# Seven products for chunk 0 too, a fourth exponential buffer for the eighth pair, and a last store in halves

## The chip, the cores and the metric

The kernel runs on one core of a Trainium2 chip. The metric is the device time of one execution in microseconds (us). A core has five engines with a queue of instructions each: TensorE (PE; its weight loads are listed as PEld), VectorE (DVE), ScalarE (ACT), GpSimd (POOL) and SyncE (SP). SP, ACT and POOL also start transfers (DMAs). The time before is the median of five runs: 339.68 us (338.87 to 341.57).

## What is computed

Block-causal attention over 8 batches, 8 heads, 576 positions and 64 elements per head, followed by two large products with an activation between them:

```python
def _attn_ref(q, k, v):
    scores = (1.0 / np.sqrt(D)) * np.matmul(q, k.transpose(0, 1, 3, 2))
    mask = block_i >= block_j              # blocks of 64 positions
    scores = np.where(mask, scores, -1000000000.0)
    attn = np.exp(scores - np.max(scores, axis=-1, keepdims=True))
    attn = attn / (np.sum(attn, axis=-1, keepdims=True) + 1e-09)
    return np.matmul(attn, v)

x = attn_out.transpose(0, 2, 1, 3).reshape(4608, 512)
h = x @ w_in                               # 512 x 2048
g = h * (1.0 / (1.0 + np.exp(-beta * h)))
out = g @ w_out                            # 2048 x 512
```

## The kernel before

**Pairs.** The attention is done in 32 pairs of heads, four to a batch: pair u is batch u // 4. For each pair, Q and K are loaded, cast to bf16 and turned (batches 0 and 1 on TensorE, line 624, with a copy on DVE, line 632; later ones by a transposing DMA, line 660). Then come the scores on TensorE (line 692), the exponentials on ACT (lines 706 and 718) into a buffer of the class E, small memsets on DVE for the mask, the product with V on TensorE (line 744), the norm on DVE (lines 756 and 763), and a transpose into xT (batches 0 to 2 on TensorE, line 783, with copies on lines 791 and 793; later ones by DMA, line 770).

**Chunks.** The rest is done in nine chunks of 512 rows. Chunk r needs all pairs of the batches in which its rows lie: chunk 0 needs batch 0, chunk 1 batches 0 and 1, chunk 2 batches 1 and 2, and so on. Its hidden part has 16 groups of four products of 128x512 (line 955); after each group ACT takes the tanh (line 965) and DVE makes a slice of gT (line 969). The out part multiplies gT with w_out.

**Out part, plain.** Chunk 0 alone: four row blocks w, for each 16 products of 128x512 in one bank of PSUM (line 991), a copy by ACT (line 1006) and a store of 256 KB from the ACT queue (line 1012). Its products need w_out only as far as each has got.

**Out part, Strassen.** The chunks listed in FAST (line 378), 1 to 8, cut gT and w_out into quarters and take seven products of quarters instead of eight. Each of the seven is two halves of eight products of 128x256 (line 885). They need sums and differences of gT's quarters (line 852, eight instructions on DVE for a chunk, some in place, some in the tensor OV) and of w_out's (function weights, line 832, eight instructions, once; one quarter of w_out is changed in place, after all plain products). OV shares its memory with a buffer for V of batch 1, so these also wait for that buffer's casts. The results are gathered in three accumulators, Z, W and Y, one bank of PSUM each: ACT copies out of Z (line 900) and DVE adds to the copy from W or Y (line 903). Four blocks are stored per chunk, 256 KB each, from the ACT queue (line 910).

**Buffers.** There are three E buffers (NE = 3). A fourth, of the class EX, lies in the memory of gT[1], the gT buffer of chunk 1; only pair 3 uses it (line 665). So the slices of chunk 1's gT wait for the users of that tile, which is remembered as `spare` (lines 733 and 971). PSUM has eight banks: scores take pairs of banks from (0, 2), the V product a pair from the list `pv.at` (line 736), and single tiles (P1) banks 4 to 7 while pairs are still to be placed, all eight afterwards.

**Order.** All work is entered as operations with dependences, buffers, an estimated duration and a priority. A planner (class Plan) plays them through in its own estimated time and fixes the order in each engine's queue: at each step the ready operation with the lowest priority number goes first. The number is 1000 + 100 r + j for hidden group j of chunk r; for Strassen halves 16 + 0.1 k above the chunk's base for the first two, and above 103 for the others, so that these lie among the next chunk's hidden groups; 10 u for pairs 4 to 7; and 994 + 100 (b - 1.5) + 4.9 c for pair c of a later batch b. `after` and `rest` of a store hold it back behind another operation or for a time. In the last chunk (`fin`) all halves follow at once.

Of the kernel before, what the change touches and what calls it, by code (L numbers as in the profile page):

```python
# [4 lines left out]
ACT = mybir.ActivationFunctionType  # L5
ALU = mybir.AluOpType
# [11 lines left out]
NRC = NROWS // RC  # L18
# [337 lines left out]
def bass_blockwise_causal_attn__then__act_swish_beta_kernel(  # L356
# [10 lines left out]
    with es:  # L367
# [7 lines left out]
        GROUPS = [((0,), (1,), (2,), (3,))] + [((0, 1), (2, 3))] * 7  # L375
        NS = 6
        NO = 4
        FAST = range(1, NRC)
        RX = 5 * RC
        OV = sb("OV", [128, 5120], f32)  # L380
        ST = [sb(f"ST{i}", [128, 36, 64], f32) for i in range(2)]
# [5 lines left out]
        TW = {k: OVh[:, k - 2] for k in (2, 3, 4)}  # L387
# [20 lines left out]
        ost = [sb(f"ost{i}", [128, DM], f32) for i in range(NO)]  # L408
        warm = sb("warm", [128, 2], f32)
        PS = es.enter_context(nc.psum_tensor("PS", [128, 8, 512], f32))  # L410
# [4 lines left out]
        P = Plan()  # L415
# [11 lines left out]
        def dve_t(n):  # L427
            return (n + 125) / 0.96
# [16 lines left out]
        def mk(fn):  # L445
# [4 lines left out]
            out=identF[:], in_=identF[:], compare_op=ALU.not_equal, fill=1.0, base=0,  # L450
# [3 lines left out]
            out=identB[:], in_=identB[:], compare_op=ALU.not_equal, fill=1.0, base=0,  # L454
# [5 lines left out]
        for i in range(NQ):  # L460
# [5 lines left out]
            o = P.op("POOL", 200, mk(lambda g, i=i: g.memset(Vn[i][:, 4, :, 64:66], 0.0)), prio=-5)  # L466
# [6 lines left out]
        for i in range(NQ, NE + 1):  # L473
# [4 lines left out]
                  xfer=100, dma=("d_beta", 1), prio=0.1)  # L478
# [28 lines left out]
        for i in range(NFILL):  # L507
# [10 lines left out]
            n = 215 if i < 12 else 110  # L518
            o = P.op("PE", n, ff, deps=[c2, c4], tiles=[tf], lat=n, mode="full", prio=1e6 + i)
# [6 lines left out]
        for b in range(B):  # L526
# [4 lines left out]
            for h0, h1, e, tt in PARTS[b]:  # L531

                vs = []
                for i in tt:
# [9 lines left out]
                    n = (h1 - h0) / 8 * (1 if i < 4 else 0.25)  # L544
# [46 lines left out]
        for u in range(NU):  # L591
            b, c = divmod(u, NPAIR)
# [69 lines left out]

                turned = [P.op("SP", 3250, ft, deps=casts, tiles=[tt_, tn], xfer=3200, prio=-1, dma=["d_T", 0, 1])]
            tqk, cps = tt_, turned
            te = P.tile("EX" if u == 3 else "E")
            ex = []
            zs = []
            qk = {}
# [61 lines left out]
                    a = 1024 * g0 + 512 * h + off + 128 * i - 128 * t  # L730
                return Ef[es_(te)][:, a:a + 128]

            if u == 3:
                spare = te
            pv = P.tile("PP")
            pv.at = (4, 6, 0, 2) if u == 3 else (4, 6) if b < 1 else (0, 2)
            ti, tx = P.tile("inv"), P.tile("xq")

            def fav(g, e, te=te, pv=pv, Tv=Tv, c=c):
# [98 lines left out]
        def fast(r, row, tg, gs):  # L838
            if not tw:
                weights()  # L840
            fin = r == NRC - 1
            old = [o for t in early for o in t.users] if r == FAST[0] else []
            t2, t3 = P.tile("S2"), P.tile("S3")
            NP = 2
            SZ = HJ // NP

            def G(a, b, i=None):
                x = gT[tg.slot][:, HJ * b:HJ * b + HJ, HC * a:HC * a + HC]
                return x if i is None else x[:, SZ * i:SZ * i + SZ]
# [13 lines left out]
            for i in range(NP):  # L863
                o = comb(lambda i=i: G(1, 0, i), lambda i=i: G(1, 0, i), lambda i=i: G(1, 1, i), ALU.add, i,
                         gs[SZ * i:SZ * i + SZ] + gs[HJ + SZ * i:HJ + SZ * i + SZ] + [SS[3][i]], [tg])
                o.same = gs[SZ * i:SZ * i + SZ] + gs[HJ + SZ * i:HJ + SZ * i + SZ]
                SS[3][i].same = gs[SZ * i:SZ * i + SZ]
                SS[1].append(o)
            for i in range(NP):
                o = comb(lambda i=i: piece(SW[2], i), lambda i=i: G(1, 0, i), lambda i=i: G(0, 0, i), ALU.subtract, i,  # L870
                         [SS[1][i]] + old, [tg, t2])
                o.same = [SS[1][i]]
                SS[2].append(o)

            def out_rows(a, b):
                return out[row + HC * a:row + HC * a + HC, HM * b:HM * b + HM].rearrange("(w p) n -> p w n", p=128)

            step = [0]

            def prod(ps, fa, fb, deps, tiles, first, last):  # L880
                z = []
                for w in range(2):
                    def fp(g, e, w=w):
                        for j in range(HJ):
                            x = g.matmul(PS[:, ps.slot, HM * w:HM * w + HM], fa()[:, j, 128 * w:128 * w + 128],  # L885
                                         fb()[:, j, :], start=first and w == 0 and j == 0, stop=last and w == 1 and j == HJ - 1,
                                         skip_group_check=True)
                        return x

                    k = step[0]  # L890
                    step[0] += 1
                    n = HJ * mm(HM)
                    z.append(P.op("PE", n, fp, deps=deps, tiles=[ps, tg, *tiles], lat=n + 170, mode="full",
                                  prio=1000 + 100 * r + (16 + 0.1 * k if fin or k < 2 else 103 + 16 / 12 * (k - 2))))
                z[1].after = z[0]
                return z

            def evac(ps, to, deps, add=None, same=()):
                if add is None:
                    return P.op("ACT", act_t(DM) + 80, lambda g, e: g.activation(  # L900
                        ost[to.slot][:], PS[:, ps.slot, :], ACT.Copy, scale=0.5),
                        deps=deps, tiles=[ps, to], lat=act_t(DM) + 160, prio=0)
                o = P.op("DVE", dve_t(DM), lambda g, e: g.scalar_tensor_tensor(  # L903
                    out=ost[to.slot][:], in0=PS[:, ps.slot, :], scalar=0.5, in1=ost[add.slot][:],
                    op0=ALU.mult, op1=ALU.add), deps=deps, tiles=[ps, to] + ([add] if add is not to else []), prio=0)
                o.same = list(same)
                return o

            def store(to, a, b, x, after=None, rest=0.0):
                o = P.op("ACT", 500, lambda g, e: [g.dma_start(  # L910
                    out_rows(a, b), ost[to.slot][:].rearrange("p (w n) -> p w n", w=2))],
                    deps=[x], tiles=[to], xfer=900, dma=["d_ost", to], prio=-1)
                o.after, o.rest = after, rest
                return o

            Z, W, Y = P.tile("P1"), P.tile("P1"), P.tile("P1")
            oz, ou, ot, oc = (P.tile("ost") for _ in range(4))
            wl, wh = wout[0:2], wout[2:4]
            lo, hi = gs[0:HJ], gs[HJ:NJ]
            p1 = prod(Z, lambda: G(0, 0), lambda: quad(w_out, 0, 0), lo + wl, [], True, False)  # L920
            z1 = evac(Z, oz, p1)
            p2 = prod(W, lambda: G(0, 1), lambda: quad(w_out, 1, 0), hi + wh, [], True, True)
            c11 = evac(W, oz, p2 + [z1], add=oz)
            for i in range(NP):
                o = comb(lambda i=i: G(0, 1, i), lambda i=i: G(0, 1, i), lambda i=i: piece(SW[2], i), ALU.subtract, i,
                         [SS[2][i]] + p2 + hi, [tg, t2])
                o.same = [SS[2][i]] + hi
                SS[4].append(o)
            p6 = prod(Z, lambda: SW[2], lambda: TW[2], SS[2] + tw[2] + [z1], [t2], False, False)
            u2 = evac(Z, ou, p6)  # L930
            store(oz, 0, 0, c11, after=u2)
            p7 = prod(Y, lambda: SW[3], lambda: TW[3], SS[3] + tw[3], [t3], True, False)
            p5 = prod(Z, lambda: G(1, 0), lambda: quad(w_out, 0, 1), SS[1] + tw[1] + [u2], [], False, False)
            tt = evac(Z, ot, p5)
            c22 = evac(Y, ot, p7 + [tt], add=ot)
            p3 = prod(Z, lambda: G(0, 1), lambda: quad(w_out, 1, 1), SS[4] + [tt] + wh, [], False, True)
            c12 = evac(Z, oc, p3)
            store(oc, 0, 1, c12)
            store(ot, 1, 1, c22, after=c12)
            p4 = prod(Y, lambda: G(1, 1), lambda: TW[4], hi + tw[4] + [c22], [], False, True)  # L940
            c21 = evac(Y, ou, p4 + [u2], add=ou)
            store(ou, 1, 0, c21, rest=0.0 if fin else 1500.0)

        for r in range(NRC):
            row = RC * r
# [139 lines left out]
```

## Time and profile before

| | |
|---|---|
| median of five runs | 339.68 us |
| profiled execution | 339.68 us, of which the span of instructions 337.9 |
| granted TensorE clock | 1.00 |
| hidden products, 128x512 (L955) | 576 |
| chunk 0's out products, 128x512 (L991) | 64 |
| Strassen products, 128x256 (L885) | 896 |
| ACT tanh, 128x512 (L965) | 144 of 697 ns |
| ACT exponential, 128x1024 (L706) | 96 of about 1.03 us |
| stores (ACT queue) | 36 of 256 KB |

An instruction is named by engine, line and the tiles that it writes and reads. A matmul's listed duration runs from its start to its modelled end, so that neighbours overlap; the rate of a stream is read from the chain of waits or from start to start. The chain of waits is followed back from the last instruction to what released each step. In the list of stretches each engine's busy time stands with the number of its instructions.

### The profile page before, as it was taken

How to read it: one execution, taken by the hardware profiler on the slowest of the kernel's cores; microseconds unless marked ns; L12 is line 12 of the kernel's file. 1: busy time of each engine (PE TensorE's matmuls, PEld its weight loads, DVE VectorE, ACT ScalarE, POOL GpSimd, SP SyncE). 2: the span in 40 equal slices, each digit the busy share in tenths (PEclk: the TensorE clock that was granted, in tenths of full speed). 3: DMA queues.
4: the chain of work that ended last, by engine and by line, in shares of the span. 5: the costliest groups of instructions: out<-in, count | busy, mean ns of one | idle time of the engine just before them, and what ended most of it. 6: DMA issues, size and time to landing. Idle time of an engine off the chain costs nothing.

```text
span 337.9 us, 7534 instructions
## 1 busy us (share of the span) xinstructions
PE 328.3 (97%) x3162; PEld 206.5 (61%) x3106; DVE 222.6 (66%) x447; ACT 211.5 (63%) x314; POOL 86.1 (25%) x127
## 2 busy tenths in 40 slices
PE   7998999999999999999999999999999999999995
PEld 5575446535567556865566666567556766666684
DVE  3737867487864679737957695768376866666742
ACT  1762994189467788559777659775777545544511
POOL 7646181084083007301530352051000000000000
PEclk9999999999999999999999999999999999999999
DMA  8999999999999799999899999997021200110023
GB/s 196 223 238 228 191 223 199 191 267 214 188 247 203 163 206 207 180 187 224 165 162 229 251 199 222 195 145 159 33 53 39 83 31 33 50 45 31 23 73 126
DMA packets 154978, 53.43 MB, mean 158 GB/s; under 512 B 139056, under 2 KB 154432, under 8 KB 154944
## 3 DMA queue, kind: packets, MB, share of 16 engines
q1 hardware_dynamic: 140096, 39.14, 61.1%
q10 hardware_dynamic: 9280, 9.44, 8.8%
q0 software_dynamic: 5568, 4.36, 8.2%
q8 instruction: 25, 0.41, 0.5%
q14 instruction: 9, 0.07, 0.1%
HBM read 36.71 MB, written 9.44 MB: 137 GB/s over the span
## 4 chain that ended last, share of the span: by engine, by line
PE 91%; ACT 4%; DVE 3%; issue 1%; POOL 0%; POOLq 0%; ACTq 0%
PE PS L955 35%; PE PS L885 29%; PE PS L744 8%; PE PS L692 8%; PE PS L991 4%; PE PS L513 2%; ACT E L706 2%; DVE gT L969 2%; PE PS L515 2%; PE PS L783 1%; ACT th L965 1%; PE PS L624 1%; DVE xq L763 1%; DVE gT L852 1%; ACT xT L791 0%
## 5 line engine op out<-in xcount | busy, mean ns | idle before, releaser
L955 PE MATMUL PS<-xT,w_in 128*128 128x512 bf16 x576 | 137.5, 380 | 0.6 <-ACT xT L791 0.2
L965 ACT ACTIVATE th<-PS,beta 128x512 f32<-128x512 f32 x144 | 96.7, 697 | 59.9 <-PE PS L955 59.1
L969 DVE SCALAR_TENSOR_TENSOR gT<-th,PS 128x512 f16<-128x512 f32 x144 | 95.6, 682 | 36.9 <-ACT th L965 36.6
L706 ACT ACTIVATE E<-PS 128x1024 bf16<-128x1024 f32 x93 | 92.3, 1029 | 28.0 <-PE PS L692 26.9
L955 PEld LDWEIGHTS PS<-xT,w_in 128*128 128x128 bf16 x576 | 52.7, 98 | 56.7 <-issue 3.4
L885 PE MATMUL PS<-w_out,gT 128*128 128x256 f16 x512 | 63.2, 273 | 0.0
L885 PEld LDWEIGHTS PS<-w_out,gT 128*128 128x128 f16 x512 | 48.9, 98 | 11.4 <-issue 0.2
L564 POOL CAST Vn<-Vs 128x640 bf16<-128x640 f32 (+1 forms) x28 | 21.0, 749 | 100.9 <-DMA Vs<-in_v_dram 99.6
L653 POOL CAST QKn<-ST 128x640 bf16<-128x640 f32 x48 | 38.8, 808 | 28.0 <-DMA ST<-in_k_dram 14.0
L692 PE MATMUL PS<-QKT 64*128 64x192 bf16 (+4 forms) x328 | 37.1, 297 | 0.7 <-DVE xq L763 0.6
L744 PEld LDWEIGHTS PS<-Vn,E 128*128 128x128 bf16 x930 | 31.7, 97 | 3.8 <-DVE xq L763 0.4
L900 ACT ACTIVATE ost<-PS 128x512 f32<-128x512 f32 x32 | 19.2, 599 | 23.5 <-PE PS L885 23.4
L744 PE MATMUL PS<-Vn,E 128*128 128x65 bf16 x930 | 32.8, 193 | 0.3 <-DVE xq L763 0.3
L885 PE MATMUL PS<-OV 128*128 128x256 f16 x256 | 32.0, 273 | 0.0
L692 PEld LDWEIGHTS PS<-QKT 64*128 64x128 bf16 (+1 forms) x328 | 13.4, 95 | 27.4 <-issue 15.4
L885 PEld LDWEIGHTS PS<-OV 128*128 128x128 f16 x256 | 24.3, 98 | 6.1 <-issue 0.4
L763 DVE TENSOR_TENSOR xq<-PS,inv 128x640 bf16<-128x640 f32 x32 | 26.3, 821 | 0.8
L903 DVE SCALAR_TENSOR_TENSOR ost<-PS,ost 128x512 f32<-128x512 f32 x24 | 16.3, 681 | 14.0 <-PE PS L885 8.4
L852 DVE TENSOR_TENSOR OV<-gT 128x1024 f16<-128x1024 f16 x32 | 23.3, 738 | 0.5
L712 DVE MEMSET E<- 64x64 uint32 x62 | 6.9, 112 | 23.9 <-ACT E L706 22.1
L885 PE MATMUL PS<-OV,gT 128*128 128x256 f16 x128 | 16.0, 273 | 0.0
L991 PE MATMUL PS<-w_out,gT 128*128 128x512 f16 x64 | 15.3, 380 | 0.0
(60 smaller groups left out, 178.7 us busy)
## 6 DMA issues: line engine op xcount, KB each, us to landing
out_dram<-ost ACTq DMA_DIRECT2D x36, 256.0 KB, 3.2
ST<-in_q_dram SPq DMA_DIRECT2D x12, 576.0 KB, 6.0
ST<-in_k_dram SPq DMA_DIRECT2D x12, 576.0 KB, 8.0
Vs<-in_v_dram SPq DMA_DIRECT2D x24, 256.0 KB, 4.3
ST<-in_q_dram SPq DMA_DIRECT2D x8, 288.0 KB, 7.3
ST<-in_k_dram SPq DMA_DIRECT2D x8, 288.0 KB, 7.7
w_in<-in_moe_w_in_dram POOLq DMA_DIRECT2D x4, 512.0 KB, 10.2
w_out<-in_moe_w_out_dram POOLq DMA_DIRECT2D x4, 512.0 KB, 9.9
```

Source lines behind the costliest of these rows:

```text
L564: return g.tensor_copy(Vn[t.slot][:, 0:n, g0:g1, 0:64], Vs[ts.slot][:, 0:n, g0:g1, :])
L653: return g.tensor_copy(QKn[tn.slot][:].rearrange("p a w n -> p (a w n)")[:, 640 * (2 * a + w):][:, 0:640] .rearrange("p (t h d) -> p t h d ...
L692: z = g.matmul(o, QKT[tqk.slot][r, p, 1, 128 * t + y:128 * t + m + y], x)
L706: return g.activation(E3[es_(te)][:, g0, :, :], PS[:, ps.slot:ps.slot + 2, :], ACT.Exp, scale=0.125)
L744: z = g.matmul(o, eblk(te, t, i, h), Vn[Tv.slot][:, t, 2 * c + h, 0:65], start=(t == 0), stop=(t == i))
L763: return g.tensor_tensor(xq[tx.slot][:].rearrange("p i (h d) -> p h i d", h=2), both(pv, 0, 64), x, ALU.mult)
L852: return P.op("DVE", dve_t(SZ * HC / 2), mk(lambda g: g.tensor_tensor(fo(), fx(), fy(), op)), deps=deps, tiles=tiles, prio=prio)
L885: x = g.matmul(PS[:, ps.slot, HM * w:HM * w + HM], fa()[:, j, 128 * w:128 * w + 128], fb()[:, j, :], start=first and w == 0 and j == 0, st ...
L955: z = g.matmul(PS[:, ph.slot, :], w_in[:, c, 128 * j:128 * j + 128], xT[:, c, row % RX:row % RX + RC], start=(c == 0), stop=(c == 3))
L965: return g.activation(th[tt.slot][:], PS[:, ph.slot, :], ACT.Tanh, scale=beta[:, j:j + 1])
L969: return g.scalar_tensor_tensor(out=gT[tg.slot][:, j, :], in0=th[tt.slot][:], scalar=1.0, in1=PS[:, ph.slot, :], op0=ALU.add, op1=ALU.mult)
L991: z = g.matmul(PS[:, po.slot, 0:d1 - d0], gT[tg.slot][:, j, 128 * w:128 * w + 128], w_out[:, j, d0:d1], start=(j == 0), stop=(j == NJ - 1))
```

## The change

The diff has three parts. FAST now begins with chunk 0, so all nine chunks use Strassen's seven products, and the combined weights are made before chunk 0's. Pair 7 too uses the class EX, `spare` becomes pair 7's tile, and pair 7's V product may take any of the four pairs of banks. In the last chunk Y is two tiles, one for each half of 256 columns: the sums out of it are done by halves (new function half), the last block is stored in two DMAs, and SP issues all its stores, without the order by `after`. The pause `rest` before the last store of chunk 7 goes to zero.

```diff
-        FAST = range(1, NRC)
+        FAST = range(0, NRC)
...
-            te = P.tile("EX" if u == 3 else "E")
+            te = P.tile("EX" if u in (3, 7) else "E")
...
-            if u == 3:
+            if u == 7:
                 spare = te
             pv = P.tile("PP")
-            pv.at = (4, 6, 0, 2) if u == 3 else (4, 6) if b < 1 else (0, 2)
+            pv.at = (4, 6, 0, 2) if u == 3 else (4, 6) if b < 1 else (0, 2, 4, 6) if u == 7 else (0, 2)
...
             def prod(ps, fa, fb, deps, tiles, first, last):
                 z = []
+                pair = isinstance(ps, list)
                 for w in range(2):
-                    def fp(g, e, w=w):
+                    pw = ps[w] if pair else ps
+
+                    def fp(g, e, w=w, pw=pw):
                         for j in range(HJ):
-                            x = g.matmul(PS[:, ps.slot, HM * w:HM * w + HM], fa()[:, j, 128 * w:128 * w + 128],
-                                         fb()[:, j, :], start=first and w == 0 and j == 0, stop=last and w == 1 and j == HJ - 1,
-                                         skip_group_check=True)
+                            x = g.matmul(PS[:, pw.slot, HM * w:HM * w + HM], fa()[:, j, 128 * w:128 * w + 128],
+                                         fb()[:, j, :], start=first and (pair or w == 0) and j == 0,
+                                         stop=last and (pair or w == 1) and j == HJ - 1, skip_group_check=True)
...
+            def half(ps, to, deps, add, w):
+                n = slice(HM * w, HM * w + HM)
+                return P.op("DVE", dve_t(HM), lambda g, e: g.scalar_tensor_tensor(
+                    out=ost[to.slot][:, n], in0=PS[:, ps.slot, n], scalar=0.5, in1=ost[add.slot][:, n],
+                    op0=ALU.mult, op1=ALU.add), deps=deps, tiles=[ps, to] + ([add] if add is not to else []), prio=0)
...
-            def store(to, a, b, x, after=None, rest=0.0):
-                o = P.op("ACT", 500, lambda g, e: [g.dma_start(
-                    out_rows(a, b), ost[to.slot][:].rearrange("p (w n) -> p w n", w=2))],
-                    deps=[x], tiles=[to], xfer=900, dma=["d_ost", to], prio=-1)
-                o.after, o.rest = after, rest
+            def store(to, a, b, x, after=None, rest=0.0, w=slice(0, 2)):
+                o = P.op("SP" if fin else "ACT", 500, lambda g, e: [g.dma_start(
+                    out_rows(a, b)[:, w], ost[to.slot][:].rearrange("p (w n) -> p w n", w=2)[:, w])],
+                    deps=[x], tiles=[to], xfer=450 * (w.stop - w.start), dma=["d_ost", to], prio=-1)
+                o.after, o.rest = None if fin else after, rest
...
-            Z, W, Y = P.tile("P1"), P.tile("P1"), P.tile("P1")
+            Z, W, Y = P.tile("P1"), P.tile("P1"), [P.tile("P1"), P.tile("P1")] if fin else P.tile("P1")
...
-            c22 = evac(Y, ot, p7 + [tt], add=ot)
+            c22 = [half(Y[w], ot, p7 + [tt], ot, w) for w in range(2)] if fin else [evac(Y, ot, p7 + [tt], add=ot)]
...
-            p4 = prod(Y, lambda: G(1, 1), lambda: TW[4], hi + tw[4] + [c22], [], False, True)
-            c21 = evac(Y, ou, p4 + [u2], add=ou)
-            store(ou, 1, 0, c21, rest=0.0 if fin else 1500.0)
+            p4 = prod(Y, lambda: G(1, 1), lambda: TW[4], hi + tw[4] + c22, [], False, True)
+            if fin:
+                for w in range(2):
+                    store(ou, 1, 0, half(Y[w], ou, [p4[w], u2], ou, w), w=slice(w, w + 1))
+            else:
+                store(ou, 1, 0, evac(Y, ou, p4 + [u2], add=ou), rest=1500.0 if r < NRC - 2 else 0.0)
```

More of the change, by code (lines that the diff above doesn't have):

```diff
@@ L892, in prod @@
                     n = HJ * mm(HM)
-                    z.append(P.op("PE", n, fp, deps=deps, tiles=[ps, tg, *tiles], lat=n + 170, mode="full",
+                    z.append(P.op("PE", n, fp, deps=deps, tiles=[pw, tg, *tiles], lat=n + 170, mode="full",
                                   prio=1000 + 100 * r + (16 + 0.1 * k if fin or k < 2 else 103 + 16 / 12 * (k - 2))))
@@ L938, in fast @@
             store(oc, 0, 1, c12)
-            store(ot, 1, 1, c22, after=c12)
-            p4 = prod(Y, lambda: G(1, 1), lambda: TW[4], hi + tw[4] + [c22], [], False, True)
-            c21 = evac(Y, ou, p4 + [u2], add=ou)
-            store(ou, 1, 0, c21, rest=0.0 if fin else 1500.0)
+            store(ot, 1, 1, c22[-1], after=c12)
+            p4 = prod(Y, lambda: G(1, 1), lambda: TW[4], hi + tw[4] + c22, [], False, True)
[4 more added lines that the diff above has]
+                store(ou, 1, 0, evac(Y, ou, p4 + [u2], add=ou), rest=1500.0 if r < NRC - 2 else 0.0)
         for r in range(NRC):
```

## The prediction

> **What bounds the kernel now.** I read the page's shares and slices first, then the chain of waits, then busy time by stretch, then the order of the instructions in two places: around pair 7, and at the end.
>
> ```profile
> span 337.9 us, 7534 instructions
> PE 328.3 (97%) x3162; PEld 206.5 (61%) x3106; DVE 222.6 (66%) x447; ACT 211.5 (63%) x314; POOL 86.1 (25%) x127
> ...
> DMA  8999999999999799999899999997021200110023
> ...
> PE 91%; ACT 4%; DVE 3%; issue 1%; POOL 0%; POOLq 0%; ACTq 0%
> ```
>
> TensorE carries 91% of the chain that ended last. The DMA slices are full up to about 230 us and then nearly empty: the attention inputs arrive at the pace of the transfers, chunks of the second part (hidden and out products) fill TensorE between the pairs, and what is left runs after them.
>
> ```profile
> 55.16 0.38 PE PS L692 x6
> 55.56 1.02 ACT E L706
> ...
> 57.72 2.70 PE PS L991 x12
> 60.42 0.90 PE PS L744 x30
> ...
> 68.69 2.59 PE PS L955 x12
> ...
> 320.33 13.99 PE PS L885 x128
> ```
>
> These are pieces of the chain: start, length, what. They give the rates of a full stream: 12 hidden products of 128x512 in 2.59 us, 216 ns each; 128 Strassen products of 128x256 in 13.99 us, 109.3 ns each. Around 55.56 the chain leaves TensorE for pair 7's exponential.
>
> ```profile
> 40.59 0.76 DVE L632 COPY QKT<-PS 128x576 bf16<-128x576 bf16 x1
> ...
> 50.56 1.97 PE L744 MATMUL PS<-Vn,E 128*128 128x65 bf16 x60
> ...
> 54.96 0.56 PE L692 MATMUL PS<-QKT 64*128 64x320 bf16 x6
> ...
> 60.25 1.07 PE L744 MATMUL PS<-Vn,E 128*128 128x65 bf16 x30
> ...
> 65.07 1.03 PE L955 MATMUL PS<-xT,w_in 128*128 128x512 bf16 x4
> ```
>
> Pair 7's turned Q and K lie ready at 41.35 (the last of the 16 copies of L632), but its scores start at 54.96: all three E buffers were held until pairs 4 and 5 had been multiplied with V (50.56 to 52.5). So its V product comes at 60.25 and chunk 1's hidden products start at 65.07. Until then TensorE lives on chunk 0's plain out products: 32 of 64 (4, 12, 8 and 8 in the timeline) lie before 65.07, 6.9 us.
>
> ```profile
> 40.00:50.00 10.00, 9.87 (x57) 4.13 (x52) 6.71 (x16) 9.50 (x16) 6.52 (x9) 1.00 1.13 213
> 50.00:57.00 7.00, 6.74 (x122) 4.59 (x120) 6.31 (x15) 3.10 (x5) 2.17 (x3) 1.00 1.23 205
> 57.00:65.00 8.00, 8.00 (x73) 4.19 (x69) 3.35 (x10) 1.94 (x2) 0.00 (x0) 1.00 1.25 196
> 65.00:80.00 15.00, 14.88 (x105) 6.70 (x101) 10.81 (x20) 11.21 (x18) 8.39 (x10) 1.00 1.07 245
> 80.00:95.00 15.00, 15.00 (x126) 8.10 (x121) 11.82 (x26) 10.34 (x15) 2.86 (x3) 1.00 1.10 197
> 95.00:110.00 15.00, 14.35 (x176) 10.88 (x171) 7.92 (x21) 9.14 (x15) 8.89 (x12) 1.00 1.10 219
> ```
>
> Busy us in each stretch (PE, PEld, DVE, ACT, POOL; clock, DMA share, GB/s): TensorE is full; ACT is nearly full only from 40 to 50, DVE has least room from 50 to 57 and from 65 to 95.
>
> **What the Trainium skill says.** TensorE: Matmul & The Clock Gate, "Back-to-back issue gap", gives N/2.4 + 2.5 ns for a warm array: 215.8 ns for 512 columns and 109.2 for 256. The trace agrees (216 and 109.3). DMA: Bandwidth & Descriptors, "Anatomy of one DMA — SWDGE (gpsimd) path", fits about 2.0 us of fixed cost to a DMA of the GpSimd path, most of it the receipt of the write, so halving a store can't halve its landing; this trace's late stores land in 2.2 to 2.6 us, of which my packet sum below leaves about 1.5 fixed. PSUM — Partial Sum Buffer, "PSUM bank collisions raise a hardware error", demands that a reader takes another bank than the matmul writes: that is why halves of the last sum need two banks. No run here shows a collision.
>
> **The change, part by part.**
>
> Chunk 0's products. Removed: 64 of 128x512, 64 x 216 = 13.8 us. Added: 7 x 16 = 112 of 128x256, 112 x 109.3 = 12.2 us. TensorE gains 1.6 us. DVE gains 8 combinations of 0.69 us (L852's median), 5.5 us, and 3 sums of 0.69 (L903), 2.1 us; ACT keeps 4 copies (0.60 each). Stores stay four of 256 KB. The eight weight combinations (L832, about 6 us) are only moved from in and behind chunk 0 to ahead of its later products: they need all of w_out, whose last quarter lands at 48.50 + 13.7 = 62.2. DVE from 50 to 110 holds about 40 us of work by the rows above; with 7.6 more it is at about 80%. Between 120 and 140, where Strassen chunks already run, it holds 16.1 of 20 us and TensorE is full there, so I price the load at nothing. What hides the wait for the combined weights is chunk 1's hidden work, 64 x 216 = 13.8 us of it; without that cover it costs what the slower rival below says.
>
> Pair 7's fourth buffer. Its scores can follow pair 6's, whose exponentials end at 47.47, instead of waiting for 52. Its three wide exponentials and the short one (3 x 1.02 + 0.22 = 3.3 us) then fall where ACT is busy 9.5 of 10 us (40 to 50), and push chunk 0's last five tanh back by as much, to about 56; ACT is nearly idle from 52 to 66, so it catches up. The V product follows pair 6's at about 54, its norm, transposes and copies take what they take now (60.25 to 63.96, 3.7 us), so xT is complete at about 58 and hidden chunk 1 starts some 7 us earlier. That stands in for the plain products as filler. TensorE's sum from 50 to 65 closes: four V products (3.6), transposes (1.6), four or five late hidden groups of chunk 0 (4), pair 7's scores gone, products 1 of Strassen (1.8, its two quarters of w_out landed at 52.1 and 55.4), and four or more hidden groups of chunk 1 (3.5 and more). The chain's step at 55.56 (1.0 us) goes; bounds: 1.0 gained, to 1.0 lost when the displaced tanh or DVE's longer queue leave gaps between 47 and 60. I take 0.2 gained. The wait that chunk 1's gT has on the alias of gT[1] moves from pair 3 to pair 7; chunk 1 needs pair 7's xT anyway, so it adds nothing.
>
> The end. Today:
>
> ```profile
> 333.72 1.73 ACTq L910 DMA_DIRECT2D out_dram<-ost x2
> 333.81 0.49 PE L885 MATMUL PS<-OV,gT 128*128 128x256 f16 x3
> ...
> 334.34 0.69 DVE L903 SCALAR_TENSOR_TENSOR ost<-PS,ost 128x512 f32<-128x512 f32 x1 [2.45 <-PE PS L885]
> ```
>
> Product 4 ends at 334.30, the sum takes 0.69, the store is issued at about 335.06, the span ends at 337.9. Split, the first half's sum and store run beside the second half's eight products (0.87 us). A 256-wide sum has no row; 512 takes 0.68 to 0.69 and 640 (L763) 0.82, a slope of about 1.1 ns per element, so about 0.40: 0.29 gained. A store's half is 128 packets of 1 KB; the page's q10 gives 8.8% x 16 x 337.9 / 9280 = 51 ns per packet, over 16 engines 0.41 us for 128: 0.41 gained. Bounds: nothing, if the landing is all fixed cost, to 0.7. SP takes over all four blocks' stores of the last chunk, five DMAs; its queue has nothing left but the wait for the stores (71.4 us of it in the list of waits), and each issue takes about 0.4, so the one for the first half (about 333.9) is out before the last (about 334.8). The other sum now takes two halves, about 0.1 longer, beside product 3. Total for the end: 0.7.
>
> The pause of 1.5 us before chunk 7's last store falls away: it moves one issue, worth nothing either way.
>
> Sum: 339.68 (the profiled execution: span 337.9 and 1.8 around it) - 1.6 - 0.2 - 0.7 = 337.2. The profiled execution is also the median of the five.
>
> **Rivals.** "Cannot be told from no change" is within 0.5%, 338.0 to 341.4.
>
> A, the attention sets the pace. Hidden chunk 2 starts at 109.28, when batch 2's last xT copy is done, and by then, counted in the timeline, 160 of the 176 out products of chunks 0 and 1 are through: 16, or 1.75 us, are in hand. Taking 1.6 us of work away leaves 0.15. If the pairs come no earlier and the remaining products wait for sums, TensorE idles instead, and only the end's 0.7 is won: 339.0. For it: full DMA slices. Against: 24 products in hand at chunk 3's start (145.4), 80 at chunk 4's, so only two places are tight, and pairs move up when TensorE is freer.
>
> B, slower. Pair 7 does not come forward (its scores are placed behind the V products because PSUM pairs, not E, hold it), and hidden chunk 1 still starts at 65. Until then only products 1 are free of combined weights; 6.9 us of filler are replaced by 1.75, 5.2 lost against 2.3 won: 342.6. It decides once chunk 1 starts later than about 61. Against: both score banks are free at 47.5, and its V product may use two more bank pairs.
>
> C, the front gains more: the gaps before 110 (0.65 us in the last row, some of the waits on ACT near 73) close as well; 335.5.
>
> **Numbers.** Forecast 0.64, A 0.15, B 0.13, C 0.08. The forecast's own range, with the end from 0 to 0.7 or a little more and the front 1.0 either way, is 335.8 to 338.9. The range 335.4 to 339.6 takes C and A in and leaves B and edges out. Faster by over 0.5%: four fifths of the forecast and C, 0.60; within: the rest of the forecast and A, 0.27; slower 0.13.
>
> **What would show it.** In the changed profile: L885 x1008 and no L991; pair 7's scores before 50; the first hidden product of chunk 1 near 58; no gap of TensorE over half a us between 55 and 75, and at 105 to 110; last matmul 1.6 to 2 us earlier; from it to the end about 2.9 instead of 3.6. I am wrong if hidden chunk 1 starts after 61, or if TensorE idles before chunk 2.

## The result

| | before | after |
|---|---|---|
| median of the compared runs | 339.6 us (337.4 to 343.1) | 340.43 us (338.47 to 342.86) |
| ratio, with 95% interval | | 1.0025 [1.0008, 1.0041] |
| profiled execution | 339.68 us, span 337.9 | 338.79 us, span 337.0 |

No gain. The time lies above the range (335.4 to 339.6), on the side that 0.27 was given to: within half a per cent. A second measurement of the same kernel, further down, gave 0.9992 [0.9966, 1.0018]. In every kernel some executions have a mean granted clock of 0.995 or less, instead of 0.998 or more, and mostly take 1 to 2 us longer; at full clock alone the second measurement is 339.45 us against 338.67, a ratio of 1.0023, close to the 1.0025 of the first.

So the changed kernel is not faster, and is probably about a quarter of a per cent slower.

The profiled execution is quicker than the median of its kernel by 1.6 us. It is one draw: chunk 0's hidden part begins at 31.0 us in it and at 31.9 in the profile of before, and in the profiles of all kernels below this start lies anywhere between about 30 and 32.5. So the profile tells where the time lies, and the medians how much it is.

The page of the changed kernel, the totals and the first line of its chain of waits:

```profile
span 337.0 us, 7638 instructions
PE 327.8 (97%) x3210; PEld 210.5 (62%) x3154; DVE 229.1 (68%) x460; ACT 211.8 (63%) x314; POOL 86.1 (26%) x127
...
PE 86%; DVE 7%; ACT 5%; issue 1%; POOL 0%; POOLq 0%
```

DVE's part of the chain rose from 3 to 7%, TensorE's fell from 91 to 86. DVE's busy time rose by 6.5 us only, 2% of the span. Where it rose is the point. Busy us by stretch in the changed kernel (PE, PEld, DVE, ACT, POOL; clock, DMA share, GB/s):

```profile
57.00:65.00 8.00, 7.78 (x51) 4.38 (x51) 7.55 (x18) 3.73 (x6) 0.00 (x0) 1.00 1.16 214
65.00:80.00 15.00, 14.45 (x134) 8.96 (x128) 14.33 (x24) 10.30 (x15) 9.95 (x11) 1.00 1.09 214
80.00:95.00 15.00, 14.24 (x138) 9.45 (x134) 10.55 (x22) 8.54 (x15) 1.90 (x3) 1.00 1.19 223
95.00:110.00 15.00, 14.84 (x205) 11.44 (x198) 8.84 (x23) 7.93 (x12) 8.28 (x11) 1.00 1.10 223
```

From 65 to 80 DVE is busy for 14.33 of 15 us, 96% (10.81 before), from 57 to 65 for 7.55 of 8 (3.35 before). TensorE, almost full there before (14.88 of 15), has holes. The timeline of the changed kernel shows two of them (start, length, engine, what; in brackets the idle time before and what ended it):

```profile
74.34 1.05 PE L888 MATMUL PS<-OV 128*128 128x256 f16 x8 [0.44 <-DVE OV L832]
...
77.05 2.23 POOL L653 CAST QKn<-ST 128x640 bf16<-128x640 f32 x2 [0.62 <-DMA ST<-in_q_dram]
77.49 1.20 DVE L832 TENSOR_TENSOR OV<-w_out,OV 128x1024 f16<-128x1024 f16 x1
77.60 1.07 PE L744 MATMUL PS<-Vn,E 128*128 128x65 bf16 x30
...
78.90 0.91 DVE L832 TENSOR_TENSOR OV<-w_out,OV 128x1024 f16<-128x1024 f16 x1
...
80.03 0.22 DVE L756 RECIPROCAL inv<-PS 128x10 f32<-128x10 f32 x1
80.28 0.82 DVE L763 TENSOR_TENSOR xq<-PS,inv 128x640 bf16<-128x640 f32 x1
...
81.75 0.53 PE L783 MATMUL PS<-identB,xq 128*128 128x128 bf16 x5 [0.76 <-DVE gT L981]
```

At 74.34 a product of chunk 0 waits for its combined weights. The second hole takes one step more to read. Pair 8's V product ends near 78.6. Its norm, which needs a fifth of a microsecond for the reciprocal, starts at 80.03, because two weight combinations (77.49 and 78.90) and two small memsets are ahead of it in DVE's queue. TensorE's queue has the transpose of that norm next and stands until 81.75. The wait ended with a slice of gT (L981, 81.02 to 81.70), which comes right behind the norm in DVE's queue: both are late by the two combinations ahead of them. In the kernel before, the V product of the same pair came at the same time, its norm followed at once, and the transpose had no wait:

```profile
77.49 1.07 PE L744 MATMUL PS<-Vn,E 128*128 128x65 bf16 x30
...
78.62 0.22 DVE L756 RECIPROCAL inv<-PS 128x10 f32<-128x10 f32 x1
...
80.25 0.52 PE L783 MATMUL PS<-identB,xq 128*128 128x128 bf16 x5
```

To compare kernels I added up all such holes of TensorE: each matmul counts with its own rate, the rest is wait, and matmul records missing from a trace are allowed for. These sums are estimates; the differences between kernels say more than the levels.

| TensorE waits, us | before | after | after, again |
|---|---|---|---|
| 40 to 57 | 1.3 | 1.9 | 2.5 |
| 57 to 95 | 1.8 | 3.9 | 4.5 |
| 95 to 110 | 1.8 | 1.3 | 1.3 |
| 40 to 110, sum | 4.9 | 7.1 | 8.3 |
| 110 to 270, sum | 7.2 | 7.3 | 7.2 |

TensorE's own work after 30 us fell from 284.2 to 282.0 us. The 1.6 us from chunk 0's products are in that. Between 40 and 110 the waits grew by 2.2 us, by 3.4 in the second profile, and take it back. Of this growth 0.6 and 1.2 us lie ahead of 57, where transposes of the last pairs wait for norms, and 2.1 and 2.7 between 57 and 95. From chunk 0's first hidden group to chunk 8's it is 266.6 us before, 267.4 and 268.4 after.

The end, in the timeline of the changed kernel:

```profile
332.35 1.91 PE L888 MATMUL PS<-OV,gT 128*128 128x256 f16 x16
...
333.42 0.42 DVE L903 SCALAR_TENSOR_TENSOR ost<-PS,ost 128x256 f32<-128x256 f32 x1 [1.51 <-PE PS L888]
334.29 0.42 DVE L903 SCALAR_TENSOR_TENSOR ost<-PS,ost 128x256 f32<-128x256 f32 x1 [0.45 <-PE PS L888]
```

The last product ends at 334.26 and the span 2.74 us later; before it was 334.30 and 3.6. So in these two executions the whole 0.9 us lies behind the last product, and nothing ahead of it, in spite of the earlier start.

### The profile page after: what moved, and what is told of

It is laid out like the page before. It is cut to its first block, busy times and chain, and to the rows that moved or that the text cites. A ratio compares the mean times of both kernels' runs of the same rounds, so it can differ in the third digit from the quotient of the medians.

```text
span 337.0 us, 7638 instructions
## 1 busy us (share of the span) xinstructions
PE 327.8 (97%) x3210; PEld 210.5 (62%) x3154; DVE 229.1 (68%) x460; ACT 211.8 (63%) x314; POOL 86.1 (26%) x127
## 4 chain that ended last, share of the span: by engine, by line
PE 86%; DVE 7%; ACT 5%; issue 1%; POOL 0%; POOLq 0%
PE PS L967 34%; PE PS L888 31%; PE PS L692 8%; PE PS L744 7%; PE PS L513 2%; ACT th L977 2%; ACT E L706 2%; DVE gT L981 2%; PE PS L515 1%; PE PS L783 1%; DVE xq L763 1%; DVE OV L832 1%; DVE OV L852 1%; DVE QKT L632 1%; PE PS L624 1%
## 5 line engine op out<-in xcount | busy, mean ns | idle before, releaser
L981 DVE SCALAR_TENSOR_TENSOR gT<-th,PS 128x512 f16<-128x512 f32 x144 | 96.2, 682 | 37.6 <-ACT th L977 36.6
L706 ACT ACTIVATE E<-PS 128x1024 bf16<-128x1024 f32 x90 | 89.1, 1027 | 25.1 <-PE PS L692 23.7
L888 PE MATMUL PS<-w_out,gT 128*128 128x256 f16 x576 | 71.4, 273 | 0.1
L888 PEld LDWEIGHTS PS<-w_out,gT 128*128 128x128 f16 x576 | 54.8, 98 | 13.8 <-issue 1.1
L909 ACT ACTIVATE ost<-PS 128x512 f32<-128x512 f32 x36 | 21.6, 601 | 33.7 <-PE PS L888 33.7
L888 PE MATMUL PS<-OV 128*128 128x256 f16 x288 | 36.5, 273 | 0.4 <-DVE OV L832 0.4
L744 PEld LDWEIGHTS PS<-Vn,E 128*128 128x128 bf16 x900 | 30.1, 97 | 4.3 <-ACT E L706 0.8
L888 PEld LDWEIGHTS PS<-OV 128*128 128x128 f16 x288 | 27.1, 98 | 8.0 <-issue 1.1
L852 DVE TENSOR_TENSOR OV<-gT 128x1024 f16<-128x1024 f16 x36 | 25.5, 719 | 1.7 <-PE PS L888 1.2
L888 PE MATMUL PS<-OV,gT 128*128 128x256 f16 x144 | 18.0, 273 | 0.0
L888 PEld LDWEIGHTS PS<-OV,gT 128*128 128x128 f16 x144 | 13.9, 98 | 2.5 <-issue 0.2
```

The lines of the kernel that those rows point to most:

```text
L706: return g.activation(E3[es_(te)][:, g0, :, :], PS[:, ps.slot:ps.slot + 2, :], ACT.Exp, scale=0.125)
L744: z = g.matmul(o, eblk(te, t, i, h), Vn[Tv.slot][:, t, 2 * c + h, 0:65], start=(t == 0), stop=(t == i))
L888: x = g.matmul(PS[:, pw.slot, HM * w:HM * w + HM], fa()[:, j, 128 * w:128 * w + 128], fb()[:, j, :], start=first and (pair or w == 0) and ...
L981: return g.scalar_tensor_tensor(out=gT[tg.slot][:, j, :], in0=th[tt.slot][:], scalar=1.0, in1=PS[:, ph.slot, :], op0=ALU.add, op1=ALU.mult)
```

## The experiments

Six theories, by the letters that the expectations use. **W**: DVE, loaded with sums and weight combinations ahead of chunk 0's products, makes TensorE wait, and that eats the saving. **P**: the attention sets the pace, so work taken from TensorE comes back as idle time wherever the pairs arrive (rival A). **X**: pair 7's early exponentials cost more than they bring. **T**: the stores by SP or the end in halves cost. **O**: any change of operations makes the planner write other queues, and each order has its own waits. **S**: one kind of such waits, norms torn apart: the planner leaves 70 ns between reciprocal and multiply, and a long DVE instruction gets in. Every set has its own runs of the kernel before (medians 339.12, 339.6 and 339.46 us).

### One part at a time

Strassen for chunk 0 alone, no fourth buffer for pair 7, end as before:

```diff
-        FAST = range(1, NRC)
+        FAST = range(0, NRC)
```

> Chunk 0 with seven products alone; pair 7 in an E buffer and the end as before. Theory W (the sums on DVE ahead of chunk 0's products make TensorE wait between 57 and 95 and eat the 1.6 us saved): ratio 0.999 to 1.005, waits of TensorE between 57 and 110 at least 1.5 us longer than before. Rival P (the attention sets the pace, the saving is lost at the starts of chunks 2 and 3 or later): 0.998 to 1.001, TensorE idle in front of the first hidden group of chunk 2 or 3. As predicted blind for this part: 0.995.

345.47 us, ratio 1.0187 [1.0156, 1.0219], slower than any of the theories had it (W up to 1.005). The timeline and the stretches of this kernel:

```profile
62.31 0.64 PE L783 MATMUL PS<-identB,xq 128*128 128x128 bf16 x5 [1.18 <-DVE xq L763]
63.97 4.90 PE L963 MATMUL PS<-xT,w_in 128*128 128x512 bf16 x11 [1.02 <-DVE xT L793]
```

```profile
57.00:65.00 8.00, 5.21 (x61) 3.67 (x61) 6.29 (x16) 2.54 (x3) 0.00 (x0) 0.84 1.16 208
65.00:80.00 15.00, 13.28 (x78) 6.61 (x75) 11.44 (x19) 8.41 (x13) 10.46 (x12) 0.86 1.27 211
```

Hidden chunk 1 (L963 in this kernel) starts at 63.97, TensorE has run out of products that need no combined weights, and its waits from 57 to 65 are 3.35 us, 0.19 before. The granted clock is 0.50 from 62.5 to 69.3 us (0.84 and 0.86 are the means of the two stretches), so products there take twice as long: 6.8 us at half speed are an estimated 3.4 us, about half of the loss (the profiled execution, like all four, has a mean clock of 0.99). The rest fits the slower rival's mechanism, under the condition that it was given: chunk 1 later than about 61. The fall of the clock was in no forecast.

The fourth buffer for pair 7 alone:

```diff
-            te = P.tile("EX" if u == 3 else "E")
+            te = P.tile("EX" if u in (3, 7) else "E")
...
-            if u == 3:
+            if u == 7:
                 spare = te
...
-            pv.at = (4, 6, 0, 2) if u == 3 else (4, 6) if b < 1 else (0, 2)
+            pv.at = (4, 6, 0, 2) if u == 3 else (4, 6) if b < 1 else (0, 2, 4, 6) if u == 7 else (0, 2)
```

> Pair 7 in the fourth buffer alone; chunk 0 plain, the end as before. Theory W: nothing lost here, 0.998 to 1.001, since the plain products fill TensorE as before. Rival X (pair 7's early exponentials in front of chunk 0's last tanh cost the time): 1.003 or more. Rival P: 1.000.

340.06 us, ratio 1.0025 [1.0006, 1.0044]: a little slower, where 0.2 us of gain was forecast, and between what W (up to 1.001) and X (1.003 or more) had. Between 40 and 110 its waits are 5.1 us (before 4.9), so X as "early exponentials leave gaps at once" doesn't hold. From 110 to 270 they are 8.0 (7.2), and one hole makes up most of that, in a place where the code is the same as before:

```profile
132.76 0.22 DVE L756 RECIPROCAL inv<-PS 128x10 f32<-128x10 f32 x1
132.90 1.12 DVE L852 TENSOR_TENSOR gT<-gT 128x1024 f16<-128x1024 f16 x1
133.94 0.81 DVE L763 TENSOR_TENSOR xq<-PS,inv 128x640 bf16<-128x640 f32 x1
...
134.81 0.54 PE L692 MATMUL PS<-QKT 64*128 64x320 bf16 x6 [0.85 <-DVE xq L763]
```

Pair 15's norm is torn apart: the reciprocal is done, then comes a sum of another chunk, then the multiply, and the scores that take over the norm's banks stand. The code of that place is unchanged, so it was the new order of the queues that put the sum there: O, in the form S. That this one wait is the whole loss isn't shown; further down it goes, and the time hardly changes.

The end alone (sums by halves, the last chunk's stores by SP, no pause):

```diff
-                o = P.op("ACT", 500, lambda g, e: [g.dma_start(
+                o = P.op("SP" if fin else "ACT", 500, lambda g, e: [g.dma_start(
...
-            c21 = evac(Y, ou, p4 + [u2], add=ou)
-            store(ou, 1, 0, c21, rest=0.0 if fin else 1500.0)
+            if fin:
+                for w in range(2):
+                    store(ou, 1, 0, half(Y[w], ou, [p4[w], u2], ou, w), w=slice(w, w + 1))
...
```

> The last chunk's halves and SP's stores, and the pause of chunk 7's last store, alone. All theories that put the loss in the front: 0.7 to 0.9 us faster, 0.997 to 0.998, the span after the last product about 2.8 us instead of 3.6. Rival T (SP's stores cost what the halves win, or the planned order of the last chunks changes for the worse): 1.000 or more.

338.7 us, ratio 0.9992 [0.9972, 1.0012]: between 0.95 us gained and 0.4 lost. A cost over 0.4 us is out; T in its weaker form, no gain (1.000), lies inside the interval. In the profile the last sum (0.42) ends at 334.81 and the span at 337.1, 2.3 us later; before it took 2.9.

The fourth buffer and the end, chunk 0 plain (the edit is to the changed kernel, as in what follows):

```diff
-        FAST = range(0, NRC)
+        FAST = range(1, NRC)
```

> The change without chunk 0's seven products: the fourth buffer and the end in halves. Theory W: 0.996 to 0.999, faster than the whole change by more than 0.3%. Rival X: 1.001 or more.

339.6 us, ratio 1.0009 [0.999, 1.0028]; the wait of pair 15 stands at 135.8 (1.09 us). W had 0.996 to 0.999 here and missed. Set beside this, the whole change adds only chunk 0's Strassen: from 1.0009 to 1.0025 or, in the second measurement, 0.9992. That is 0.5 us more or 0.6 less, where the forecast had 1.6 less.

### What takes back chunk 0's gain

Chunk 0's eight sums of gT left out, the rest of the changed kernel as it is:

```diff
             def comb(fo, fx, fy, op, i, deps, tiles, prio=0.5):
+                if r == FAST[0]:
+                    return gs[-1]
...
-            p6 = prod(Z, lambda: SW[2], ...
+            p6 = prod(Z, lambda: G(1, 0) if r == FAST[0] else SW[2], ...
-            p7 = prod(Y, lambda: SW[3], ...
+            p7 = prod(Y, lambda: G(0, 0) if r == FAST[0] else SW[3], ...
```

> The whole change, but chunk 0's seven products take gT's quarters as they are, so that its eight sums on DVE (5.5 us) are left out (chunk 0's rows are then not the reference's). Theory W: TensorE's waits between 40 and 110 fall by 1 to 2 us, ratio 0.995 to 0.999. Rival O: 1.001 to 1.004.

337.68 us, ratio 0.9942 [0.9924, 0.9961]. The forecast was 337.2. With the sums that were priced at nothing the kernel is 1.7 to 2.8 us slower, by the two measurements of the changed kernel. In the two profiles the difference is 2.1 us; 0.6 of it is an earlier start of chunk 0, and 1.5 lie between chunk 0's and chunk 8's first hidden group (265.9 us, 267.4 with the sums). Its stretches, and the same norm of pair 8 in its timeline:

```profile
65.00:80.00 15.00, 14.87 (x139) 9.72 (x136) 13.68 (x25) 10.28 (x15) 10.46 (x12) 1.00 1.12 226
80.00:95.00 15.00, 15.00 (x147) 9.98 (x143) 9.76 (x21) 9.41 (x15) 2.62 (x5) 1.00 1.15 235
```

```profile
76.74 1.07 PE L744 MATMUL PS<-Vn,E 128*128 128x65 bf16 x30
...
77.85 0.22 DVE L756 RECIPROCAL inv<-PS 128x10 f32<-128x10 f32 x1 [0.48 <-PE PS L744]
78.10 0.82 DVE L763 TENSOR_TENSOR xq<-PS,inv 128x640 bf16<-128x640 f32 x1
...
79.97 0.52 PE L783 MATMUL PS<-identB,xq 128*128 128x128 bf16 x5
```

DVE is still busy for 91% from 65 to 80, but the last weight combination is through before the V product ends: now DVE waits 0.48 us for TensorE, and the transpose, with no wait, comes 1.8 us earlier, of which 0.9 is the V product's own earlier start. The waits from 40 to 110 are 5.7 us (7.1). This also speaks against P: with the same pairs and the same transfers, a kernel that stops less for DVE is 2 us faster. One caution: the edit also frees products from waiting for the sums, and gives a new order of the queues.

The other half of the load: chunk 0 takes raw quarters of w_out, and the eight weight combinations are made after its products, for chunk 1:

```diff
-            if not tw:
+            if not tw and r:
                 weights()
+            raw = r == FAST[0]
+            tw_ = {k: [] for k in (1, 2, 3, 4)} if raw else tw
...
-            p6 = prod(Z, lambda: SW[2], lambda: TW[2], SS[2] + tw[2] + [z1], [t2], False, False)
+            p6 = prod(Z, lambda: SW[2], lambda: quad(w_out, 0, 0) if raw else TW[2], SS[2] + tw_[2] + wout + [z1], [t2], False, False)
```

and likewise for products 7, 5 and 4.

> The whole change, but chunk 0's seven products take w_out's quarters as they are, and the eight combinations of w_out are made after them (chunk 0's rows are then not the reference's; the number of products is the same). Theory W (DVE is full between 57 and 80, and TensorE waits for combined weights and for norms behind them): DVE in 65 to 80 falls from 14.3 us to 9 to 12, TensorE's waits between 40 and 110 from 7.1 us to about 5.5, the time by 1 to 1.6 us, ratio 0.996 to 0.999. Rival O (each new order of the queues brings its own waits, whatever DVE has to do): waits within 0.7 of the whole change's, ratio 1.001 to 1.004.

342.61 us, ratio 1.0076 [1.0039, 1.0114], where W had 0.996 to 0.999: a miss. Its stretches, and one line of its timeline:

```profile
65.00:80.00 15.00, 15.00 (x141) 9.86 (x137) 9.59 (x19) 9.93 (x16) 9.40 (x12) 1.00 1.14 231
...
95.00:110.00 15.00, 12.10 (x158) 8.59 (x151) 11.80 (x25) 7.35 (x10) 7.49 (x8) 0.89 0.94 187
```

```profile
102.42 2.32 PE L890 MATMUL PS<-OV 128*128 128x256 f16 x16 [1.95 <-DVE OV L832]
```

Where the load was taken away, it did what W says: DVE 14.33 to 9.59 us from 65 to 80, TensorE's waits from 65 to 95 from 3.25 to 1.45. The sums stayed (DVE is busy for 7.29 of 8 us from 57 to 65), so each half of the load may go alone and TensorE is full from 65 to 95. But the combinations now come at 93.94 to 105.9, and chunk 1's products wait for them, 2 us in one place, and from 103.8 to 107.2 the granted clock is 0.50 (0.89 is the mean of the stretch). So the time of this kernel can't speak for W or against it; its stretches ahead of 95 speak for it. Neither of the two places tried for the eight combinations is free: before chunk 0's later products they collide with sums and norms, after them with chunk 1.

Four of chunk 0's eight sums on GpSimd, which is idle from 57 to 65:

```diff
-                return P.op("DVE", dve_t(SZ * HC / 2), mk(lambda g: g.tensor_tensor(
-                    fo(), fx(), fy(), op)), deps=deps, tiles=tiles, prio=prio)
+                return P.op("POOL" if pool else "DVE", 2400 if pool else dve_t(SZ * HC / 2), mk(lambda g: g.tensor_tensor(
+                    fo(), fx(), fy(), op)), deps=deps, tiles=tiles, prio=30 if pool else prio)
```

> The whole change, with four of chunk 0's eight sums (2.7 us of DVE) moved to GpSimd, which is idle from about 54 to 68; estimated at up to 2.4 us each there. Theory W (DVE's load ahead of chunk 0's products is what ate the saving): faster than the whole change by 0.3 to 0.6%, ratio 0.996 to 1.000, TensorE's waits between 40 and 110 down from 7.1 to 5.5 to 6.5. Against W: 1.001 or more, because the four sums come too late for their products, or slow DVE's own two-input instructions beside them.

340.21 us, ratio 1.0014 [0.9986, 1.0043], beside 0.9992 [0.9966, 1.0018] of the unaltered changed kernel. W had a gain of 0.3 to 0.6% and missed. Its timeline and stretches:

```profile
52.52 2.44 POOL L852 TENSOR_TENSOR gT<-gT 128x1024 f16<-128x1024 f16 x1
...
58.22 4.32 POOL L852 TENSOR_TENSOR OV<-gT 128x1024 f16<-128x1024 f16 x2
```

```profile
57.00:65.00 8.00, 7.48 (x50) 4.37 (x52) 5.24 (x14) 3.27 (x5) 5.38 (x3) 1.00 1.24 175
65.00:80.00 15.00, 14.06 (x123) 8.26 (x120) 14.57 (x22) 9.88 (x15) 10.64 (x12) 1.00 1.14 215
```

DVE has 2.3 us less from 57 to 65, but from 65 to 80 it is as full as before (14.57), for the eight weight combinations stay where the planner put them, from 64.8 to 81.4, with the last two ahead of pair 8's norm as before; its transpose waits 1.30 us, until 83.39. So W fits if the one full stretch counts and not DVE's total, but that reading came after the result. The direct test, all of the load kept and only the combinations placed behind pair 8's norm, wasn't run.

The changed kernel a second time, beside it:

> The changed kernel again, for a second profile. If the first profile (338.8, below the median of 340.4) was a lucky draw, this one lies between 339.5 and 341.5, and its difference sits in the start before chunk 0 or in waits on transfers, not in 57 to 95, where the waits on DVE are the same within 0.3 us.

339.47 us, ratio 0.9992 [0.9966, 1.0018], with the same holes at 74.3 (0.70 us) and 82.1 (1.33 us). Its profiled execution (338.89 us) lies below the expected 339.5, and its waits from 57 to 95 are 0.6 us above the first profile's, twice what was allowed. The holes come back in the same places; their size is good to about half a us.

### Norms kept together

In the profile of before, 10 of 32 norms have another instruction between reciprocal and multiply; in the changed kernel, in the one with the fourth buffer alone and in the one with buffer and end, it is 15. This edit makes the planner place them back to back, in the changed kernel:

```diff
-                    s.ready = max(s.ready, o.end + self.SEM)
+                    s.ready = max(s.ready, o.end + (0.0 if s.tight else self.SEM))
...
+            m.tight, m.prio = True, -1
```

> The whole change, with the planner told that a norm's multiply may follow its reciprocal without a pause and ahead of other work, so that no combination or gT slice is put between the two (15 of 32 pairs have one there). Theory S (that pause lets a long DVE instruction in, the pair's xq, and so its PSUM banks and xT, come 0.7 to 1.2 us later, and TensorE waits): waits of TensorE after 40 fall by 1 to 2 us, ratio 0.994 to 0.999. Rival O: no clear gain, 0.999 to 1.004.

340.96 us, ratio 1.003 [1.0008, 1.0052]; no norm is torn apart any more, and the waits from 40 to 110 are 8.4 us, not less. S doesn't explain the changed kernel.

The same edit with the fourth buffer and the end, chunk 0 plain:

> Chunk 0 plain, the fourth buffer for pair 7, the end in halves, norms kept together. Theory S (the fourth buffer's own loss is the 1.0 us wait at 134.8 behind a split norm of pair 15): the wait is gone, ratio 0.994 to 0.997. Rival O: another wait takes its place, 0.999 to 1.002.

339.63 us, ratio 1.0002 [0.998, 1.0024]. The wait of pair 15 is gone, as S says, but a new one of 1.42 us at 203.2 and smaller ones from 145 to 149 stand in its place: waits from 110 to 270 are 9.7 us, more than with the torn norms. O in general, then, and S only its instance.

And with the end alone, chunk 0 plain and pair 7 in an E buffer:

> Chunk 0 plain and pair 7 in an E buffer as before, the end in halves, and norms kept together as in the kernel above (10 of 32 pairs are split before). Theory S: 0.994 to 0.998, a little faster than the end in halves alone. Rival O: 0.998 to 1.003.

338.04 us, ratio 0.9949 [0.9917, 0.9981], faster than the kernel before and the changed one. The same kernel, measured again beside other runs of the kernel before:

> Norms kept together, the end in halves, the rest as before, a second time, for its interval: 0.993 to 0.997 if the first result holds; 0.998 or more would make it chance.

337.89 us, ratio 0.9937 [0.9909, 0.9965]. It is faster than before both times, but by less than these numbers say: at full clock the ratios are 0.9958 and 0.9977, and the end alone has 0.9992, so that keeping the norms together is worth an estimated 0.5 to 1.2 us. Why this order is better than the others isn't settled: its waits from 40 to 270 are 12.7 us, against 12.1 of before, and yet from the first product of chunk 0's hidden part to that of chunk 8's it takes 266.0 us in the first profile (before 266.6).

## Why the prediction was wrong

**The step that failed** is the price of chunk 0's DVE load: "with 7.6 more it is at about 80%. Between 120 and 140 … TensorE is full there, so I price the load at nothing." The load itself was right: from 50 to 110 DVE is busy for 47.9 us of 60 in the changed kernel, 80%. What failed is the spreading of it over 60 us. Of the 7.7 us more, 4.2 fall between 57 and 65 and 3.5 between 65 and 80, and there the weight combinations, "only moved", are stretched out: six of the eight ran from 63.88 to 70.5 before and two near 94, all eight now run from 64.21 to 79.8, among the sums. Five of them now lie beside GpSimd's casts and take 4.8 us together, where five at 0.68 would take 3.4. The stretch is 96% full and its queue runs in a fixed order, so norms and combined weights that TensorE's queue is about to need come late. From 57 to 95 TensorE waits 2.1 and 2.7 us longer in the two profiles, more than the 1.6 us saved.

That DVE's work causes these waits is shown from two sides: without the sums, and likewise without the combinations, TensorE is busy for at least 29.87 of the 30 us from 65 to 95 (28.69 with both), and without the sums the time comes to 0.9942, near the forecast's 0.993. How much of the time is the load and how much the order that the planner happened to make isn't separated. The comparison with 120 to 140 misled: the load there is 80% too, but without weight combinations. And the signs that the prediction set itself looked for holes from 55 to 75 and from 105 to 110; the largest, at 81.75, lies between.

**TensorE's work**: right, 1.6 us less. It just wasn't the end's time: the last product ends at 334.26 instead of 1.6 to 2 us earlier. The rates hold, too, but the section that the prediction names for them says something else: in the Trainium skill, TensorE: Matmul & The Clock Gate, "Back-to-back issue gap" calls this formula the gap of an isolated matmul and gives about 131 ns for 512 columns in a sustained stream. The full stream in the chain of the kernel before runs at 216 ns.

**Pair 7's fourth buffer**: the mechanism was right. In the timeline its V product is the one that reads gT, the fourth buffer's memory:

```profile
48.58 0.39 PE L692 MATMUL PS<-QKT 64*128 64x512 bf16 x2
...
53.52 1.07 PE L744 MATMUL PS<-Vn,gT 128*128 128x65 bf16 x30
...
60.10 5.34 PE L967 MATMUL PS<-xT,w_in 128*128 128x512 bf16 x24
```

Its scores run at 42.77 and 48.58, its V product at 53.52 (forecast about 54, behind pair 6's, which now comes after it at 55.17), and hidden chunk 1 starts at 60.10 (forecast 58; the turn to the slower rival put at 61). Without it chunk 0's Strassen costs 1.9%, of which an estimated half is the fallen clock. The price "0.2 gained" was wrong: alone, the buffer gave 1.0025 [1.0006, 1.0044], about 0.85 us lost, at a norm of pair 15 that the working had not looked at. The bounds of 1.0 either way held it. In the changed kernel no such wait stands there; its waits from 110 to 270 are those of before.

**The end**: right in kind. The sum's half took 0.42 for the forecast 0.40 and saved 0.27 us; the store saved 0.58 where 0.41 was forecast; from the last product to the end 2.74 where 2.9 was. Measured alone it is 0.9992 [0.9972, 1.0012], about 0.3 us, with the forecast's 0.7 inside the interval.

**The rivals.** A gave the time nearest to both measurements (339.0), but not for its reason, so that is luck: no wait over 0.35 us lies between 82 and chunk 2's start at 112.0, and from 110 to 270 the waits are as before. B's mechanism exists and is kept off by the fourth buffer. That a load priced at nothing takes the place of the work removed was no rival, though DVE's room from 50 to 57 and from 65 to 95 was named as the least.

**The range** was too narrow in the first place for that reason. In hindsight: had DVE's load been bounded from both sides, by nothing and by half of its 7.6 us (an arbitrary share), the upper end would have stood at 337.2 + 3.8 = 341. The buffer and the end played a part as well: with these two alone, chunk 0 plain, the kernel was at 1.0009, where the forecast for them had 0.9 us of gain.

**Still open**: how much of the loss is DVE's load and how much the planned order; what the combinations alone, placed behind pair 8's norm, would give; and why norms kept together help clearly in one order out of three.

## What to carry to other kernels

Price load that is added to an engine in the stretch where it will run, together with what the change moves there, and not as a share of a longer time: with queues in a fixed order, what is lost is decided by who stands behind the new instructions, and a short one on the way of the full engine (here a reciprocal of 0.2 us) can matter more than its length. When a kernel's order is planned, any edit draws a new order whose waits may be as large as the gain in question, far from the edited place; measure the parts alone and look for the largest new hole before a cause is named. In this kernel a saving on the engine that bounds came out at the end only as far as its suppliers had room.

## What the runs showed of the hardware

- DVE's sums of two f16 tensors of 128x1024 take 0.68 us, but up to 1.10 and 1.20 where GpSimd casts run beside them (72.06 and 77.49 in the changed kernel), and those casts take up to 1.1 us each instead of 0.75. The Trainium skill, SBUF — State Buffer, "SBUF: two separate sides", says that a DVE instruction with two inputs in SBUF and a GpSimd instruction that reads SBUF share a pair of ports, and that the second one waits for the whole of the first. The trace agrees that the two slow each other; waiting and sharing can't be told apart by it. Five of the eight weight combinations now run from 72 to 80 us, beside those casts.
- The same sum on GpSimd takes 2.1 to 2.4 us, three times DVE's.
- The granted clock is either 1.00 or, for a time, 0.50: from 62.5 to 69.3 us in the kernel with Strassen for chunk 0 alone, among waits of 3.35 us from 57 to 65; from 103.8 to 107.2 with raw weights for chunk 0, right behind the wait of 2 us at 102. All four and all five executions of these two kernels have a mean clock of 0.995 or less. It also comes in other kernels, in some executions: in the second profile of the norms kept together with the end alone it is 0.50 from 29.3 to 32.7 us. Such 3.4 us are a mean of 0.995 over the span and an estimated 1.7 us lost; the changed kernel's executions at 0.995 have a median of 341.69 us, the others 340.02. What sets it off isn't shown.
